# ReLU²-attention into a SwiGLU feed-forward on one core: last keys transposed apart, transposes and normalisation moved in the first batches

## The chip, the cores and the metric

The kernel runs on one core of a Trainium2 chip. The metric is the device time of one execution, in microseconds. The engines named below are TensorE (PE), VectorE (DVE), ScalarE (ACT), GpSimd (POOL, which here only issues loads) and SyncE (SP, which issues stores and transposing DMAs). Each engine executes its own instructions in program order and waits on semaphores for the others.

## The reference

Inputs are q, k, v of shape 8 x 12 x 448 x 64 (batch, heads, sequence, head size) and the weights of a feed-forward block with 768 model columns and 1536 hidden columns.

```python
scores = scale * np.matmul(q, k.transpose(0, 1, 3, 2))
attn = np.maximum(scores, 0.0) ** 2 / S
attn_out = np.matmul(attn, v)
x = attn_out.transpose(0, 2, 1, 3).reshape(B * S, H * D)
xn = x / np.sqrt(np.mean(x * x, axis=-1, keepdims=True) + 1e-06) * rms_g
g = xn @ w_gate
out = (g * sigmoid(g) * (xn @ w_val)) @ w_out
```

There is no softmax: the scores are cut at zero and squared.

## The kernel before

**Attention.** A stage `m` (0 to 23) handles four heads of one batch `b = m // 3`, as two pairs of heads; a head pair fills the 128 partitions of a transposed tile. Stages 0 to 2 are batch 0, stages 3 to 5 batch 1. `scores` (L266) makes seven score tiles per stage, called slots: slots 0 to 2 are keys 0 to 383 of the first pair in three chunks of 128, slots 3 to 5 the same of the second pair, and slot 6 holds the last 64 keys of both pairs. Each slot is a pair of 448-wide matmuls per head (into `psS`, two buffers), a ReLU on ACT (L291) and a square on DVE (L292). `attend` (L295) multiplies the seven squared tiles of the previous stage with the values, ACT copies the two results to `xT` (L327) and DVE squares them (L328).

**Transposes.** Scores need q and k with the head size on partitions. For the first two batches `transposes(n)` (L198) does that on PE for one head pair: fourteen small matmuls for q into `psQ` (where they are due), six for the 384 main keys and two for the last 64 keys into `psK`. DVE copies `psQ` to `QT` (L210) and `psK`, 448 wide, to `KT` (L223). A matmul of a slot waits until the copy that wrote its keys is done. From batch 2 on the keys (and from the second pair of batches on the queries too) come by transposing DMAs on SP, issued by the call with `j == 2`; for those batches `transposes` puts nothing else on PE beyond the q of batches 2 and 3.

**Feed-forward.** After the third stage of a batch its `norm` (L345) sums the squares with six matmuls into `psSS`, takes the root on ACT (L357), and appends to a list `bg` four reciprocals (L370) and six scalings to `xn` (L373) for DVE, and then the generation of the gate, value and output pieces. `fill` (L464) issues pieces of gates (L400, with SiLU on ACT, L408), values (L414, with a product on DVE, L421) and output projections (L443) between the slots of the attention, by a budget of time, one `bg` step with each piece.

**Order.** There is no planner: the loop at L483 writes the order out by hand, and each engine follows it. In stage `m`: slots 0 and 1; `attend(m-1)`; slots 2 and 3; fill; `norm` in stages 3, 6, 9 and so on; slots 4 and 5; `transposes(2m+2)`; fill; slot 6; `transposes(2m+3)`; fill. In stage 3 there is nothing to fill with yet, and all of `bg` is issued at the stage's end. In stages 1 to 3 `warm` (L260) puts two spare matmuls on a tile of ones ahead of each of the slots 2 to 5, one ahead of `attend`; eight stand at the start and eight in stage 4 after slots 0 and 1.

**PSUM.** `psQ`, `psK`, `psAV`, `psSS`, `psG`, `psV`, `psO` and the spare matmuls' tile take turns in four buffers with the tag `rot`.

**Loads.** POOL issues them in program order: heads 0-1 of q and k, then heads 2-3, 4-7 and 8-11, with the last 64 keys of all twelve heads (`load_kx`) ahead of the keys of heads 2-3.

Of the kernel before, what the change touches and what calls it, by code (L numbers as in the profile page):

```python
# [9 lines left out]
BF16 = mybir.dt.bfloat16  # L10
# [5 lines left out]
def kernel(  # L16
# [11 lines left out]
    nc = tc.nc  # L28
    P = nc.NUM_PARTITIONS

    B, H, S, D = q.shape
# [5 lines left out]
    XT0 = NCH * P  # L37
    XK = S - XT0
# [7 lines left out]
    ND = HP // 2  # L46
# [12 lines left out]
    psum = ctx.enter_context(  # L59
        tc.tile_pool(name="psum", bufs=2, space=bass.MemoryType.PSUM)  # L60
    )
# [15 lines left out]
    q_t, k_t, kx_t, v_t, vx_t = {}, {}, {}, {}, {}  # L77
# [14 lines left out]
    def load_q(pr, h0=0, h1=H, es=(0, 1)):  # L92
        for e in es:
            dst = q_t[pr][e * HALF : (e + 1) * HALF]
            src = q[2 * pr + e, h0:h1]
            if pr < 2:
                nc.gpsimd.dma_start(
                    out=dst[:, h0:h1],
                    in_=src.rearrange("h (p u) d -> p h u d", u=NU),
                )  # L100
            else:
                nc.gpsimd.dma_start(
                    out=dst, in_=src.rearrange("h (p u) d -> p u h d", u=NU)
                )

    def load_k(b, h0=0, h1=H):
        src = k[b, h0:h1, 0:XT0]
        if b < 2:
            nc.gpsimd.dma_start(
                out=k_t[b][:, h0:h1],  # L110
                in_=src.rearrange("h (p c) d -> p h c d", c=NCH),
            )
        else:
            nc.gpsimd.dma_start(
                out=k_t[b][:], in_=src.rearrange("h (p c) d -> p c h d", c=NCH)
            )

    def load_kx(b, h0=0, h1=H):
        nc.gpsimd.dma_start(
            out=kx_t[b][:, h0:h1], in_=k[b, h0:h1, XT0:S].rearrange("h p d -> p h d")  # L120
        )
# [15 lines left out]
    def load_gv(lo, hi):  # L137
        nc.gpsimd.dma_start(out=wg_sb[:, :, lo:hi], in_=wg_d[:, :, lo:hi])
        nc.gpsimd.dma_start(out=wv_sb[:, :, lo:hi], in_=wv_d[:, :, lo:hi])
# [6 lines left out]
    ident = const_pool.tile([P, P], BF16, name="ident", tag="ident")  # L146
    masks.make_identity(nc, ident[:])
    load_q(0, 2, 4, (0,))
    load_kx(0)
    load_k(0, 2, 4)  # L150
    load_v(0, 0, 4)
    eps_col = const_pool.tile([P, 1], FP32, name="eps_col", tag="eps_col")
    nc.vector.memset(eps_col[:], eps)  # L153
# [21 lines left out]
    def step():  # L175
        if bg:
            bg.pop(0)()


    QT, KTt, R, XT, X2 = {}, {}, {}, {}, {}  # L180
# [8 lines left out]
    def turn(dst, src, r0, r1):  # L189

        for hh in range(2):
            nc.tensor.transpose(  # L192
                out=dst[hh * D : (hh + 1) * D],
                in_=src(hh)[r0:r1],
                identity=ident[r0:r1, r0:r1],
            )

    def transposes(n):  # L198


        b, j = divmod(n, HP)
        pr, e = divmod(b, 2)
        if pr == 0 or pr == 1 and e == 0:
            r0, r1 = (e * HALF, (e + 1) * HALF) if pr == 0 else (0, P)
            if j == 0 and e == 0:
                big(pr, None)
            ps = psum.tile([P, NU, r1 - r0], BF16, name="psQ", tag="rot", bufs=4)
            for u in range(NU):
                turn(ps[:, u, :], lambda hh: q_t[pr][:, 2 * j + hh, u, :], r0, r1)
            nc.vector.tensor_copy(out=QT[pr][:, j, :, r0:r1], in_=ps[:])  # L210
        if b < 2:
            if j == 0:
                big(None, b)
            ps = psum.tile([P, S], BF16, name="psK", tag="rot", bufs=4)
            for c in range(NCH):
                turn(
                    ps[:, c * P : (c + 1) * P],
                    lambda hh: k_t[b][:, 2 * j + hh, c, :],
                    0,
                    P,  # L220
                )
            turn(ps[:, XT0:S], lambda hh: kx_t[b][:, 2 * j + hh, :], 0, XK)
            nc.vector.tensor_copy(out=KTt[b][:, j], in_=ps[:])  # L223
        if j == 2 and b > 0 and b + 1 < B:
            if e == 1 and pr > 0:
                big(pr + 1, None)
                for u in range(NU):
                    nc.sync.dma_start_transpose(
                        out=QT[pr + 1][:, :, u, :],
                        in_=q_t[pr + 1][:, u].rearrange("p h d -> p (h d)"),  # L230
                    )
            big(None, b + 1)
            for c in range(NCH):
                nc.sync.dma_start_transpose(
                    out=KTt[b + 1][:, :, c * P : (c + 1) * P],
                    in_=k_t[b + 1][:, c].rearrange("p h d -> p (h d)"),
                )
            nc.sync.dma_start_transpose(
                out=KTt[b + 1][:, :, XT0:S],
                in_=kx_t[b + 1][:].rearrange("p h d -> p (h d)"),  # L240
            )
        if j == HP - 1:
            if b + 2 < B:
                k_tile(b + 2)
                load_k(b + 2)
                load_kx(b + 2)
            if e == 0 and pr + 1 < B // 2:
                q_tile(pr + 1)
                load_q(pr + 1)
            if b == 0:  # L250
                load_gv(768, 1024)
                load_gv(1024, F)


    W: dict = {}

    def warm_tile():
        W["ps"] = psum.tile([P, S], FP32, name="psW", tag="rot", bufs=4)

    def warm(k):  # L260
        for _ in range(k):
            nc.tensor.matmul(  # L262
                out=W["ps"][:], lhsT=ones_bf[:, :P], rhs=ones_bf[:], start=True, stop=True
            )

    def scores(m, slots, k=0):  # L266
        b, t = divmod(m, ND)
        qt, kt = QT[b // 2], KTt[b]
        for s in slots:
            warm(k)  # L270
            ps = psum.tile([P, 2, 512], FP32, name="psS", tag="psS")
            if s < 2 * NCH:
                i, c = divmod(s, NCH)
                todo = [(2 * t + i, slice(0, P), slice(c * P, (c + 1) * P))]
            else:
                todo = [
                    (2 * t + i, slice(i * XK, (i + 1) * XK), slice(XT0, S))
                    for i in range(2)
                ]
            for j, rows, keys in todo:  # L280
                for hh in range(2):
                    prt = slice(hh * D, (hh + 1) * D)
                    nc.tensor.matmul(  # L283
                        out=ps[rows, hh, :S].rearrange("k (u x) -> k u x", u=NU),
                        lhsT=kt[prt, j, keys],
                        rhs=qt[prt, j, :, b % 2 * HALF : (b % 2 + 1) * HALF],
                        start=True,
                        stop=True,
                    )
            r = rpool.tile([P, 2, S], BF16, name="r", tag="r")  # L290
            nc.scalar.activation(out=r[:], in_=ps[:, :, :S], func=ACT.Relu)  # L291
            nc.vector.tensor_tensor(out=r[:], in0=r[:], in1=r[:], op=ALU.mult)  # L292
            R[m, s] = r
# [170 lines left out]
    def fill(us, idle_steps=3):  # L464

        nonlocal debt
        debt += us
        while pieces and debt > 0:
            cost, fn = pieces.pop(0)
            fn()  # L470
            debt -= cost
            step()
        if not pieces:
            debt = 0.0
            for _ in range(idle_steps):
                step()


    N = B * ND
    warm_tile()  # L480
    warm(8)
    transposes(0)
    for m in range(N + 1):  # L483
        rate = 7.8 if m < 2 * ND + 1 else 13.8
        first = m == ND
        idle = 2 if m <= ND else 0
        if m <= ND + 1:
            warm_tile()
        if m < N:
            scores(m, (0, 1))  # L490
        if m == ND + 1:
            warm(8)
            fill(0.36 * rate)
        if m > 0:
            warm(idle // 2)
            attend(m - 1)
        else:
            transposes(1)
        if m < N:
            scores(m, (2, 3), idle if m > 0 else 0)  # L500
        if not first:
            fill(0.36 * rate)
        if m > 0 and m % ND == 0:
            norm(m // ND - 1)
        if m < N:
            scores(m, (4, 5), idle if m > 0 else 0)
        if m + 1 < N:
            transposes(2 * m + 2)
        if not first:
            fill(0.36 * rate)  # L510
        if m < N:
            scores(m, (6,))
        if m + 1 < N:
            transposes(2 * m + 3)
        if first:
            while bg:
                step()
        else:
            fill(0.28 * rate)
    while pieces or bg:  # L520
# [31 lines left out]
```

## Time and profile before

| | |
|---|---|
| median of 3 runs | 476.93 us (476.84 to 477.58) |
| the profiled execution | 477.44 us, span 475.7 us |
| PE busy | 456.8 us, 96% of the span |
| DVE busy | 252.5 us, 53% |
| ACT busy | 253.6 us, 53% |
| spare matmuls (L262) | 43, 13.9 us busy |
| stage 1 begins (its slot 0 on PE) | 16.49 us |
| stage 2, stage 3, stage 4 begin | 26.04, 34.02, 43.95 us |
| first gate matmul | 48.69 us |
| `attend(3)` begins | 55.36 us |

How to read it: the profile is one execution. Its span is what the profile records, and its own time is 1.7 us more. A row of a timeline gives the start, the time from the first start to the last end of a run of like instructions, and in brackets the idle time before them with what ended it. A group's mean is the duration of one instruction; pipelined matmuls follow each other faster than that. The column PEclk is the granted clock of TensorE as a share of full speed.

### The profile page before, as it was taken

Reading aid. Unit: us, or ns where it says so; the run is one execution under the profiler, and the core shown is the slowest. Engines: PE = TensorE matmul, PEld = TensorE weight load, DVE = VectorE, ACT = ScalarE, POOL = GpSimd, SP = SyncE. Lnnn points to the kernel's source line nnn. Section 1 sums busy time; section 2 is a strip of 40 time slices with the busy share of each in tenths; the row PEclk is TensorE's granted clock in tenths of the full one; section 3 lists DMA queues with packets and bytes.
Section 4 is the critical chain, followed back from the end, with each engine's and each line's share of the span. In section 5 each row is a group of like instructions: output and inputs, shape, how many; then the busy total and the mean of one; then the engine's idle time right before and its main releaser. Section 6 shows DMA issues by size and latency. Waiting matters only on the chain.

```text
span 475.7 us, 7444 instructions
## 1 busy us (share of the span) xinstructions
PE 456.8 (96%) x3031; PEld 223.7 (47%) x3031; DVE 252.5 (53%) x428; ACT 253.6 (53%) x365; POOL 68.8 (14%) x75
## 2 busy tenths in 40 slices
PE   5988899979999999999999999999999999999996
PEld 2333344434455544444455544444455544555563
DVE  2677566785447555674446555674347552722111
ACT  3788266856474375666465375766465463422110
POOL 9653321510040003400040002000000000000000
PEclk9998899999999999999999999999999999999999
DMA  9999999999794216994294115500001210000022
GB/s 100 192 190 181 181 179 202 175 148 101 140 117 85 100 68 90 151 107 68 42 129 114 66 68 80 47 1 1 1 0 69 97 68 1 0 1 1 34 99 99
DMA packets 129282, 42.75 MB, mean 90 GB/s; under 512 B 113376, under 2 KB 125664, under 8 KB 129248
## 3 DMA queue, kind: packets, MB, share of 16 engines
q0 software_dynamic: 96336, 24.38, 61.0%
q1 hardware_dynamic: 32912, 17.90, 15.2%
q8 instruction: 23, 0.38, 0.3%
q14 instruction: 11, 0.09, 0.1%
HBM read 48.76 MB, written 11.01 MB: 126 GB/s over the span
## 4 chain that ended last, share of the span: by engine, by line
PE 86%; DVE 7%; ACT 4%; issue 1%; DMA 1%; POOL 0%; DVEq 0%; ACTq 0%; POOLq 0%
PE psO L443 23%; PE psV L414 22%; PE psG L400 22%; PE psS L283 8%; PE psAV L315 8%; ACT r L291 3%; DVE xn L373 2%; DVE r L292 2%; PE psSS L349 2%; DVE rstd L370 1%; DMA kxld<-in_k_dram 1%; PE psQ L192 1%; DVE QT L210 1%; PE psK L192 1%; DVE hT L421 1%
## 5 line engine op out<-in xcount | busy, mean ns | idle before, releaser
L291 ACT ACTIVATE r<-psS 128x896 bf16<-128x896 f32 x168 | 145.7, 921 | 39.9 <-PE psS L283 39.7
L292 DVE TENSOR_TENSOR r<-r 128x896 bf16<-128x896 bf16 x168 | 104.4, 624 | 92.3 <-ACT r L291 91.7
L400 PE MATMUL psG<-xn,wg_sb 128*128 128x448 bf16 x576 | 126.7, 353 | 4.2 <-DVE xn L373 4.1
L414 PE MATMUL psV<-xn,wv_sb 128*128 128x448 bf16 x576 | 125.9, 355 | 0.0
L443 PE MATMUL psO<-wo_sb,hT 128*128 128x384 bf16 x672 | 113.0, 326 | 0.0
L408 ACT ACTIVATE sig<-psG 128x448 bf16<-128x448 f32 x96 | 52.3, 546 | 111.5 <-PE psG L400 99.0
L421 DVE TENSOR_TENSOR hT<-sig,psV 128x448 bf16<-128x448 bf16 x96 | 59.1, 615 | 64.6 <-PE psV L414 63.1
L443 PEld LDWEIGHTS <-hT 128*128 128x128 bf16 x672 | 64.3, 98 | 46.1 <-issue 4.8
L400 PEld LDWEIGHTS <-wg_sb 128*128 128x128 bf16 x576 | 54.9, 98 | 57.7 <-issue 8.8
L414 PEld LDWEIGHTS <-wv_sb 128*128 128x128 bf16 x576 | 54.6, 98 | 56.1 <-issue 8.2
L283 PE MATMUL psS<-QT,KT 64*128 64x448 bf16 (+1 forms) x384 | 53.2, 372 | 7.2 <-DVE KT L223 4.3
L452 ACT COPY ost<-psO 128x384 f32<-128x384 f32 x28 | 13.4, 479 | 57.4 <-PE psO L443 50.3
L454 DVE COPY ost<-psO 128x384 f32<-128x384 f32 x28 | 15.6, 557 | 40.7 <-PE psO L443 40.7
L124 POOL DMA_DIRECT2D vld<-in_v_dram x10 | 9.6, 959 | 183.9 <-PE psAV L315 179.3
L283 PEld LDWEIGHTS <-KT 64*128 64x128 bf16 (+1 forms) x384 | 13.8, 97 | 40.6 <-issue 34.6
L315 PE MATMUL psAV<-r,vld 128*64 128x448 bf16 x288 | 32.8, 365 | 0.0
L373 DVE SCALAR_TENSOR_TENSOR xn<-xT,g_sb,rstd 128x448 bf16<-128x448 bf16 x48 | 31.0, 678 | 0.0
L327 ACT ACTIVATE xT<-psAV 128x448 bf16<-128x448 f32 x48 | 23.5, 542 | 4.6 <-PE psAV L315 4.4
L370 DVE RECIPROCAL rstd<-rstd 128x112 f32<-128x112 f32 x32 | 25.1, 822 | 0.0
L328 DVE TENSOR_TENSOR x<-xT 128x896 bf16<-128x896 bf16 x24 | 15.0, 625 | 15.0 <-ACT xT L327 15.0
L315 PEld LDWEIGHTS <-vld 128*64 128x64 bf16 x288 | 14.6, 111 | 16.3 <-issue 8.4
L262 PE MATMUL psW<-ones_bf 128*128 128x448 bf16 x43 | 13.9, 435 | 1.4 <-DVE eps_col L153 1.4
(34 smaller groups left out, 160.7 us busy)
## 6 DMA issues: line engine op xcount, KB each, us to landing
out_dram<-ost SPq DMA_DIRECT2D x28, 384.0 KB, 2.3
qld<-in_q_dram POOLq DMA_DIRECT2D x7, 672.0 KB, 16.8
kld<-in_k_dram POOLq DMA_DIRECT2D x7, 576.0 KB, 11.6
vld<-in_v_dram POOLq DMA_DIRECT2D x7, 576.0 KB, 7.2
wo_sb<-in_moe_w_out_dram POOLq DMA_DIRECT2D x3, 768.0 KB, 24.6
vxld<-in_v_dram POOLq DMA_DIRECT2D x16, 96.0 KB, 7.0
wg_sb<-in_moe_w_gate_dram POOLq DMA_DIRECT2D x4, 384.0 KB, 13.9
wv_sb<-in_moe_w_val_dram POOLq DMA_DIRECT2D x4, 384.0 KB, 14.1
```

What stands on the lines that cost most here:

```text
L283: nc.tensor.matmul(out=ps[rows, hh, :S].rearrange("k (u x) -> k u x", u=NU), lhsT=kt[prt, j, keys], rhs=qt[prt, j, :, b % 2 * HALF : (b % ...
L291: nc.scalar.activation(out=r[:], in_=ps[:, :, :S], func=ACT.Relu)
L292: nc.vector.tensor_tensor(out=r[:], in0=r[:], in1=r[:], op=ALU.mult)
L315: nc.tensor.matmul(out=acc[i][hh * D : (hh + 1) * D, :], lhsT=w[rows, hh, :], rhs=r[rows, hh, :], start=(c == 0), stop=(c == NCH),)
L327: nc.scalar.mul(out=xt[:, i, :], in_=acc[i][:], mul=inv_attn)
L370: nc.vector.reciprocal(out=rstd[:, sl], in_=rstd[:, sl])
L373: nc.vector.scalar_tensor_tensor(out=xn[:, kt, :], in0=xt[:, kt, :], scalar=g_sb[:, kt : kt + 1], in1=rstd[:], op0=ALU.mult, op1=ALU.mult,)
L400: nc.tensor.matmul(out=ps[:], lhsT=wg_sb[:, kt, fb * P : (fb + 1) * P], rhs=xn[:, kt, :], start=(kt == 0), stop=(kt == KT - 1),)
L408: nc.scalar.activation(out=sig[:], in_=ps[:], func=ACT.Silu)
L414: nc.tensor.matmul(out=ps[:], lhsT=wv_sb[:, kt, fb * P : (fb + 1) * P], rhs=xn[:, kt, :], start=(kt == 0), stop=(kt == KT - 1),)
L421: nc.vector.tensor_tensor(out=HT[pr, fb][:, :, e * HALF : (e + 1) * HALF], in0=st["sig"][:].rearrange("p (u x) -> p u x", u=NU), in1=ps[:] ...
L443: nc.tensor.matmul(out=ps[:], lhsT=HT[pr, fk][:, u, :], rhs=wo_sb[:, fk, o * OW : (o + 1) * OW], start=(fk == 0), stop=(fk == FT - 1),)
```

## The change

Six edits, all in how the first stages are ordered.

1. `psK` and its copy now hold only the 384 main keys. The last 64 keys of both pairs of a stage are transposed together by a new function `last_keys(m)`, into a tile `psX` (tag `rot`), and copied to `KT` by one more DVE copy. It is called in stages 0 to 5 after slots 4 and 5.
2. The load of the last 64 keys of batch 0 goes behind the keys of heads 2-3.
3. `transposes(2m+2)` goes ahead of slots 4 and 5 (in stage 0 it stays behind them).
4. In stage 3 the reciprocals and scalings are issued right behind the root, so ahead of the transposes, slots 4 to 6 and their squares.
5. In stage 4 the first fill (two gates and a value) goes ahead of slots 0 and 1.
6. Spare matmuls: two ahead of each of slots 0 to 5 in stage 0, none ahead of slots 4 and 5 in stage 3, four at the end of stage 3 in place of eight in stage 4; 47 in all.

```diff
     load_q(0, 2, 4, (0,))
+    load_k(0, 2, 4)
     load_kx(0)
-    load_k(0, 2, 4)
...
-            ps = psum.tile([P, S], BF16, name="psK", tag="rot", bufs=4)
+            ps = psum.tile([P, XT0], BF16, name="psK", tag="rot", bufs=4)
...
-            turn(ps[:, XT0:S], lambda hh: kx_t[b][:, 2 * j + hh, :], 0, XK)
-            nc.vector.tensor_copy(out=KTt[b][:, j], in_=ps[:])
+            nc.vector.tensor_copy(out=KTt[b][:, j, :XT0], in_=ps[:])
...
+    def last_keys(m):
+
+        b, t = divmod(m, ND)
+        ps = psum.tile([P, 2, XK], BF16, name="psX", tag="rot", bufs=4)
+        for i in range(2):
+            turn(ps[:, i, :], lambda hh: kx_t[b][:, 4 * t + 2 * i + hh, :], 0, XK)
+        nc.vector.tensor_copy(out=KTt[b][:, 2 * t : 2 * t + 2, XT0:S], in_=ps[:])
...
-        if m <= ND + 1:
+        if m <= ND:
             warm_tile()
+        if m == ND + 1:
+            fill(0.36 * rate)
         if m < N:
-            scores(m, (0, 1))
-        if m == ND + 1:
-            warm(8)
-            fill(0.36 * rate)
+            scores(m, (0, 1), idle if m == 0 else 0)
         if m > 0:
             warm(idle // 2)
             attend(m - 1)
         else:
             transposes(1)
         if m < N:
-            scores(m, (2, 3), idle if m > 0 else 0)
-        if not first:
+            scores(m, (2, 3), idle)
+        if first:
+            norm(0)
+            while bg:
+                step()
+        else:
             fill(0.36 * rate)
-        if m > 0 and m % ND == 0:
-            norm(m // ND - 1)
+            if m > 0 and m % ND == 0:
+                norm(m // ND - 1)
+        if m > 0 and m + 1 < N:
+            transposes(2 * m + 2)
+            if m < ND:
+                warm_tile()
         if m < N:
-            scores(m, (4, 5), idle if m > 0 else 0)
-        if m + 1 < N:
-            transposes(2 * m + 2)
+            scores(m, (4, 5), idle if m < ND else 0)
+        if m == 0:
+            transposes(2)
+        if m < 2 * ND:
+            last_keys(m)
         if not first:
             fill(0.36 * rate)
         if m < N:
             scores(m, (6,))
         if m + 1 < N:
             transposes(2 * m + 3)
         if first:
-            while bg:
-                step()
+            warm_tile()
+            warm(4)
         else:
             fill(0.28 * rate)
```

## The prediction

> **What bounds the kernel now.** I read the page first, then TensorE's waits, then the timeline of the first 60 us engine by engine, then the granted clock in short stretches.
>
> ```profile
> PE 456.8 (96%) x3031; PEld 223.7 (47%) x3031; DVE 252.5 (53%) x428; ACT 253.6 (53%) x365; POOL 68.8 (14%) x75
> ```
>
> ```profile
> PE psS L283 <- DVE KT L223: 4.3, 5, 1.1
> ...
> PE psK L192 <- DMA kxld<-in_k_dram: 1.9, 1, 1.9
> ```
>
> PE is the bound: 96% busy, and from 55 us on it hardly stops, so the end comes later by as much as PE enters that stretch later. The marker is `attend(3)`, at 55.36. Ahead of it PE waits five times for a KT copy (4.3 us) and once, at the start, for the last keys (1.9 us). The order of stages 2 and 3 on PE, DVE and ACT:
>
> ```profile
> 7.48 0.26 PE L192 MATMUL psK<-ident,kxld 64*64 64x64 bf16 x2 [1.89 <-DMA kxld<-in_k_dram]
> ...
> 26.04 0.55 PE L283 MATMUL psS<-QT,KT 64*128 64x448 bf16 x4 [0.83 <-DVE KT L223]
> ...
> 34.02 0.55 PE L283 MATMUL psS<-QT,KT 64*128 64x448 bf16 x4 [0.85 <-DVE KT L223]
> ...
> 41.88 0.38 PE L283 MATMUL psS<-QT,KT 64*64 64x448 bf16 x4 [0.41 <-ACT r L291]
> ...
> 43.95 0.93 PE L283 MATMUL psS<-QT,KT 64*128 64x448 bf16 x4 [1.03 <-DVE KT L223]
> ```
>
> ```profile
> 40.38 0.63 ACT L357 ACTIVATE rstd<-psSS,eps_col 128x448 f32<-128x448 f32 x1
> ...
> 43.51 0.38 DVE L223 COPY KT<-psK 128x448 bf16<-128x448 bf16 x1
> ...
> 44.94 2.98 DVE L370 RECIPROCAL rstd<-rstd 128x112 f32<-128x112 f32 x4
> 47.95 3.67 DVE L373 SCALAR_TENSOR_TENSOR xn<-xT,g_sb,rstd 128x448 bf16<-128x448 bf16 x6
> 51.53 1.16 DVE L292 TENSOR_TENSOR r<-r 128x896 bf16<-128x896 bf16 x2
> ```
>
> Slot 6 of stage 3 runs at 41.88, stage 4 begins at 43.95, and the normalisation, though its root is done at 41.01, is taken by DVE only at 44.94 and paces the first gate until 51.6.
>
> ```profile
> 44.00:48.00 4.00, 3.65 (x12) 1.19 (x13) 3.96 (x8) 3.01 (x3) 0.00 (x0) 0.60 1.72 182
> 48.00:51.00 3.00, 1.48 (x4) 0.38 (x4) 3.00 (x6) 0.00 (x0) 1.77 (x2) 0.94 1.27 201
> 51.00:54.00 3.00, 2.87 (x8) 1.09 (x8) 1.69 (x4) 0.54 (x1) 0.75 (x1) 0.50 1.36 175
> 54.00:56.00 2.00, 2.00 (x16) 0.91 (x16) 0.62 (x1) 0.53 (x1) 0.00 (x0) 0.99 1.51 152
> ```
>
> The columns are the stretch and its length, then busy time of PE, PEld, DVE, ACT and POOL, then the granted clock. It is 0.50 in 51 to 54, after a stretch with PE half idle, and 0.99 after 54. The pitch says the same: six value matmuls take 2.10 us of the chain at 52.20, six gate matmuls 1.14 at 54.30, so 0.36 against 0.19 us each. At the start the clock column shows 1.00, but matmuls have the slow pitch until 20.09 (eight spare ones in 3.17 us); there I go by the pitch.
>
> **The change part by part.** All times are of the profiled execution, 477.44 us (span 475.7), 0.5 above the median of 476.93.
>
> *Stage 0 (edits 1, 2, 6).* Slot 0 no longer waits for the last keys: the six main-key transposes end at 5.6, two spare matmuls (0.75) follow, the copy (about 0.35 against 0.38) is done by 6.0, so slot 0 is at 6.3 instead of 8.23. This lead of 1.9 us is lost: the keys of heads 4-7, issued at 6.67, land 6.4 us later at 13.07 (they ran at 14.43), and `transposes(2)` needs them. Behind it come the square of slot 5 and the copies QT, KT (0.30 each) and psX, then slot 6 at 14.9 (fast pitch) to 15.9 (slow), `transposes(3)` 0.6 to 0.97, and stage 1 begins at 15.8 to 16.9. I take 16.2, against 16.49. The swapped load costs nothing: the last keys land when the other load did, at 4.58 + 4.3 = 8.9, and are first needed near 13.4; without that slack `last_keys(0)` would wait up to 1.9, as before.
>
> *Stages 1 and 2 (edits 1, 3).* Let P be the beginning of a stage. As before, `attend` and two `xT` copies follow, the ReLU of slot 2 starts at P + 3.31 (26.04 to 29.35), and slot 3 leaves PE at P + 3.9. Now `transposes` (0.62 without last keys: 23.52 to 24.14) and two spares (0.48) come ahead of slot 4: P + 5.0, its ReLU at P + 5.4, 0.5 later than the spacing of 0.81 allows. The ReLU of slot 5 ends at P + 7.1. Slot 6 must now wait for the psX copy, which stands on DVE behind the square of slot 5: 0.03 + 0.62 + copy + 0.05, so P + 8.0. No row shows this copy of 128 columns; it lies between a 128x1 write (0.06) and the 448-wide copy (0.38), I take 0.2, nearer the copy. Then slot 6 (0.25) and `transposes(2m+3)` (0.62): the next stage begins at P + 8.9, where stage 2 took 7.98. What is saved is the wait of 0.83 for the KT copy; what replaces it is a PE wait of about 1.8 ahead of slot 6. Queued behind slot 6 on PE is everything, and ACT waits too.
>
> So with a fast clock stage 3 begins at 16.2 + 17.8 = 34.0, just as before (34.02). But the wait sits between two groups of transposes: from `transposes(2)` to stage 1 there are some 3.5 us with only slot 6 (0.25) as full matmuls; between stages 1 and 2 some 2.8. In the trace, 23.52 to 26.04 is such a stretch of 2.5 us and the pitch stays fast; 40.62 to 43.95 is one of 3.3 us and slots 0 and 1 come out slow (0.93 for four against 0.55). The first joint is longer than the one that dropped; I take a slow beginning of stage 1 and none after. Its price: `xT` came 20.50 - 16.49 = 4.01 after the beginning in slow stage 1 and 2.45 in stage 2, so 1.56 (bounds 0, and 2.4 if the spares ahead of slots 2 and 3 are slow too, about 0.4 for each pair). Stage 3 then begins at 35.6, 1.6 later (bounds -0.4 to +5).
>
> [...]
>
> *Stage 3 (edits 4, 6): the costly step.* Up to the root all stands as before, so it ends at 41.01 plus the delay. DVE then takes reciprocals and scalings at once (44.94 to 51.62 was 6.7): 47.7. Then come, in this order, QT and KT (0.6), the squares of slots 4 and 5 (1.16), and only then the psX copy (0.2): slot 6 runs at 49.7 instead of 41.88. ACT did its ReLUs long ago. PE has nothing to do from about 41 to 49.7 and is slow after it. Behind slot 6 are queued `transposes(9)` (0.51 + 0.46 slow, as at 9.09), four spares, two gates and a value (18 matmuls), slots 0 and 1 of stage 4. Slot 6 and transposes end at 51.1. All of xn is ready, so nothing paces the gates but the pitch. When does it become fast? The trace shows 3 us of dense matmuls (51 to 54), and 6.1 us from 13.92 to 20.0 with transposes among them; bounds 2.6 and 6, I take 4.3, their middle. At 0.37 that is 11.6 of the 22 matmuls; the other 10.4 at 0.19 take 2.0; slots 0 and 1 take 0.48: 51.1 + 4.3 + 2.0 + 0.5 = 57.9, against 55.36: 2.5 later (bounds 1.7 and 3.3). The eight spares of stage 4 and the wait for the scalings are gone in this sum; the stall has moved ahead of slot 6.
>
> *Stage 4 and later.* The ReLUs of slots 0 and 1 now stand behind the second SiLU (0.54 + two at 0.81), and slot 3 waits a little for its buffer: 0.1 (bounds 0 and 0.9, one ReLU). In stages 4 and 5 the chain to slot 6 is covered by three pieces (1.14 each) between `last_keys` and slot 6; without them it would cost the 0.9 of stage 2. Two of the moved q transposes of stages 6 to 8 (0.58 each) fall ahead of waits that exist anyway (1.39 for ACT at 98.36, 1.20 for the scalings at 102.11, whose DVE work stands in the same place): 0, bounds -0.5 and 0.5. On SP the transposing DMAs keep their sequence, on POOL only the swapped pair changes: 0; the latest gate weights land at 68.8 (40.97 + 27.8), 10 us ahead of their gate at 79.5. Six more DVE copies lie where DVE is idle, except as counted. The net of four more spares is in the sums.
>
> Sum: 1.6 + 2.5 + 0.1 = 4.2. 477.4 + 4.2 - 0.5 = 481.1.
>
> **The rivals.**
> *No slow beginning.* The clock holds between stages 0 to 3: 0.0 + 2.5 + 0.1 = 2.6, 479.5. For it: 23.52 to 26.04. Against: 43.95. [...]
> *More slow beginnings.* Stage 2 or 3 begins slow too, 1.56 each: 482.7 or 484.3. For it: 2.8 us is nearer to 3.3 than comfort; against: 2.5 held twice.
> *Faster.* The stages run at ACT's pace, because the moved copies take away the 0.91 us in which ACT waits for slot 0: 7.98 - 0.91 = 7.07 per stage. From 15.8 stage 3 would begin at 29.9, 4.1 earlier, and 4.1 - 2.6 is a gain of 1.5: 475.4. It decides if stage 3 begins before 31.4. Loads allow it (batch 1's keys land at 24.9). Against: slot 6 behind the square of slot 5, which no order on ACT can hide.
> *Small or no loss.* An early return of the fast clock in stage 3 (1.7) with part of that lead: 477 to 478.3.
>
> **How the numbers follow.** One slow beginning 0.40 (own range 479.9 to 482.4), none 0.25, more 0.22, a loss under 1.4 us 0.04, no measurable difference 0.03, faster 0.06. A measurement tells about 0.2%, 1 us, from no change. The range reaches from the no-drop case at its low norm stage and a little lead (478.3) to two further drops with a late clock (485.5); outside lie the faster, the equal and part of the small-loss case and the tail of the slow ones. Slower: 0.40 + 0.25 + 0.22 + 0.04 = 0.91.
>
> **What would show it.** Right: slot 0 near 6.3; a PE wait of 1.5 to 2 ahead of slot 6 in stages 1 and 2 put down to the psX copy; in stage 3 such a wait of 8 to 9 us, scalings done near 48 to 50; slow gates, `attend(3)` at 57 to 61. Wrong: if stage 3 begins before 31.4, or slot 6 of stage 3 doesn't wait, or PE has idle time after 60 us in which the delay vanishes.

## The result: 1.1% slower, as forecast

The changed kernel takes 481.80 us (median of 4 executions, 480.96 to 483.90), the kernel before 476.88 beside it. The ratio is 1.0108, with a 95% interval of 1.0073 to 1.0143. The forecast was 481.1, in 478.3 to 485.5. Here and below a ratio is taken over the executions that lie within 1.5% of the fastest of their kernel; this leaves out one execution of the sixth experiment and three of the tenth.

The profiled execution of the changed kernel is the slowest of its four: 483.90 us, span 482.1. So what is read from it is the costliest of four cases, 2.1 us above the median. For every execution the mean granted clock is known too; it is 0.978 in all four. The profiled execution stands 6.5 us above the profiled execution of before (477.44).

From its page, the engines' busy time, and TensorE's waits (in all, how often, the longest):

```profile
PE 458.3 (95%) x3035; PEld 223.8 (46%) x3035; DVE 252.9 (52%) x434; ACT 253.7 (53%) x365; POOL 68.8 (14%) x75
```

```profile
PE psS L290 <- DVE KT L259: 14.0, 4, 9.0
PE psG L407 <- DVE xn L380: 2.1, 3, 1.2
PE psS L290 <- ACT r L298: 1.8, 4, 0.9
```

PE's work has hardly grown (458.3 against 456.8). The wait for the last keys at the start and the waits of slot 0 for its keys are gone. One new line takes their place: four waits of slot 6 for the copy of the last keys (L259), 14.0 us, one of them 9.0. The timeline of PE shows where they are:

```profile
6.62 0.56 PE L290 MATMUL psS<-QT,KT 64*128 64x448 bf16 x2
...
15.64 0.38 PE L290 MATMUL psS<-QT,KT 64*64 64x448 bf16 x4 [1.65 <-DVE KT L259]
...
26.39 0.38 PE L290 MATMUL psS<-QT,KT 64*64 64x448 bf16 x4 [1.66 <-DVE KT L259]
...
27.21 0.36 PE L290 MATMUL psS<-QT,KT 64*128 64x448 bf16 x2
27.79 0.56 PE L290 MATMUL psS<-QT,KT 64*128 64x448 bf16 x2 [0.22 <-ACT r L298]
28.28 0.56 PE L269 MATMUL psW<-ones_bf 128*128 128x448 bf16 x1
28.77 2.45 PE L322 MATMUL psAV<-r,vld 128*64 128x448 bf16 x12
...
37.12 0.38 PE L290 MATMUL psS<-QT,KT 64*64 64x448 bf16 x4 [1.66 <-DVE KT L259]
...
37.94 1.14 PE L290 MATMUL psS<-QT,KT 64*128 64x448 bf16 x4
...
55.20 0.59 PE L290 MATMUL psS<-QT,KT 64*64 64x448 bf16 x4 [9.03 <-DVE KT L259]
```

Slot 0 runs at 6.62 instead of 8.23, but stage 1 begins at 16.46, where it began at 16.49. After each wait of 1.65 the next stage falls to the slow pitch: in stage 2 slot 0 is still fast (0.36 for two matmuls), slot 1 is slow (0.56), and the twelve matmuls of `attend` take 2.45 instead of 1.32. The same rows of the kernel before, in stages 1 and 2:

```profile
17.84 2.32 PE L315 MATMUL psAV<-r,vld 128*64 128x448 bf16 x12
...
26.82 1.32 PE L315 MATMUL psAV<-r,vld 128*64 128x448 bf16 x12
```

Stage 1 begins slow there too, at the end of the slow pitch from the start, so in stage 1 the drop takes away a gain and in stages 2 and 3 it is a loss against the kernel before. The granted clock of the changed kernel in stretches of the same execution (second column the length, then PE, PEld, DVE, ACT, POOL, then the clock):

```profile
16.60:20.00 3.40, 3.18 (x17) 1.08 (x14) 2.26 (x5) 2.02 (x3) 2.15 (x3) 0.64 1.31 205
...
26.80:30.20 3.40, 3.18 (x31) 1.31 (x27) 2.26 (x5) 2.54 (x3) 1.30 (x3) 0.65 1.55 194
...
37.00:40.00 3.00, 2.81 (x33) 1.24 (x35) 1.56 (x5) 2.42 (x3) 2.67 (x4) 0.67 1.46 196
...
51.00:54.00 3.00, 0.00 (x0) 0.00 (x0) 3.00 (x7) 0.00 (x0) 0.75 (x1) 0.50 1.43 145
```

In the kernel before the clock column of these early stretches is 1.00 up to 40 us (in its first 20 us that says little, because the column reads 1.00 at the slow pitch too, as in 6.4 to 9.8 us, where the four matmuls at 8.23 take 0.93). In 51 to 54 PE does nothing at all, and DVE is busy throughout; its timeline says with what:

```profile
46.69 2.99 DVE L377 RECIPROCAL rstd<-rstd 128x112 f32<-128x112 f32 x4 [1.32 <-ACT rstd L364]
49.71 3.67 DVE L380 SCALAR_TENSOR_TENSOR xn<-xT,g_sb,rstd 128x448 bf16<-128x448 bf16 x6
53.29 0.38 DVE L210 COPY QT<-psQ 128x448 bf16<-128x448 bf16 x1
53.59 0.35 DVE L222 COPY KT<-psK 128x384 bf16<-128x384 bf16 x1
53.86 1.15 DVE L299 TENSOR_TENSOR r<-r 128x896 bf16<-128x896 bf16 x2
54.92 0.22 DVE L259 COPY KT<-psX 128x128 bf16<-128x128 bf16 x1
```

The root ends at 46.65, the scalings follow without a gap, and the copy that slot 6 waits for comes last, 8.3 us after the root.

Four markers carry the rest of this section. Each is read from the profiled execution of its kernel; the experiments are described below.

| kernel | stages 1, 2, 3 begin | root ends | `attend(3)` begins | root to `attend(3)` | its time |
|---|---|---|---|---|---|
| before | 16.49, 26.04, 34.02 | 41.01 | 55.36 | 14.35 | 477.44 |
| changed | 16.46, 27.21, 37.94 | 46.65 | 62.25 | 15.60 | 483.90 |
| 1: normalisation late | 16.28, 27.04, 37.79 | 46.51 | 63.10 | 16.59 | 486.19 |
| 2: spares in the wait | 15.87, 25.16, 34.46 | 41.85 | 57.43 | 15.58 | 479.12 |
| 3: last keys early | 14.30, 21.73, 29.74 | 37.34 | 53.43 | 16.09 | 476.16 |
| 4: normalisation early alone | 16.59, 26.27, 34.26 | 41.25 | 57.49 | 16.24 | 481.76 |
| 5: copies first | 14.38, 22.66, 30.66 | 38.26 | 49.41 | 11.15 | 473.82 |
| 6: 5 with spares | 14.11, 21.50, 29.50 | 37.10 | 48.50 | 11.40 | 472.00 |
| 7: before, spares at the joint | 16.23, 26.22, 34.20 | 41.19 | 55.95 | 14.76 | 479.67 |
| 8: transposes in the wait | 16.11, 25.61, 35.12 | 42.50 | 58.51 | 16.01 | 480.17 |
| 9: stage 3 alone mended | 14.78, 24.52, 34.73 | 42.60 | 52.99 | 10.39 | 476.41 |
| 10: 6 with spares in the gate | 14.47, 21.86, 29.86 | 37.47 | 47.86 | 10.39 | 472.04 |
| 11: wait half filled | 15.76, 24.98, 34.20 | 41.58 | 58.71 | 17.13 | 483.05 |

Of the 6.9 us by which `attend(3)` is later in the changed kernel, 3.9 have come up by the beginning of stage 3, 1.7 more by the root (stage 3 begins slow too), and 1.25 between root and `attend(3)`. About 0.4 is given back by the end; the waits of stage 7 are 0.5 shorter, down from 1.39 + 0.44 + 1.20 + 0.25 to 0.88 + 0.44 + 1.17 + 0.25 us, because the q transposes now fill a part of the first.

### The profile page after: what moved, and what is told of

Its sections match the earlier page's. It is cut to its first block, busy times and chain, and to the rows that moved or that the text cites. A ratio compares the mean times of both kernels' runs of the same rounds, so it can differ in the third digit from the quotient of the medians.

```text
span 482.1 us, 7461 instructions
## 1 busy us (share of the span) xinstructions
PE 458.3 (95%) x3035; PEld 223.8 (46%) x3035; DVE 252.9 (52%) x434; ACT 253.7 (53%) x365; POOL 68.8 (14%) x75
## 4 chain that ended last, share of the span: by engine, by line
PE 89%; DVE 6%; ACT 3%; issue 1%; DMA 1%; POOL 0%; ACTq 0%; DVEq 0%; POOLq 0%
PE psO L450 23%; PE psV L421 22%; PE psG L407 22%; PE psS L290 8%; PE psAV L322 8%; ACT r L298 3%; DVE xn L380 2%; PE psSS L356 2%; PE psW L269 2%; DVE r L299 1%; DVE rstd L377 1%; PE psQ L192 1%; DMA kld<-in_k_dram 1%; PE psK L192 1%; DVE hT L428 0%
## 5 line engine op out<-in xcount | busy, mean ns | idle before, releaser
L322 PE MATMUL psAV<-r,vld 128*64 128x448 bf16 x288 | 35.0, 383 | 0.0
L322 PEld LDWEIGHTS <-vld 128*64 128x64 bf16 x288 | 15.2, 116 | 17.5 <-issue 10.5
L269 PE MATMUL psW<-ones_bf 128*128 128x448 bf16 x47 | 16.5, 454 | 1.4 <-DVE eps_col L153 1.4
```

Of the source, the lines that this page charges most:

```text
L269: nc.tensor.matmul(out=W["ps"][:], lhsT=ones_bf[:, :P], rhs=ones_bf[:], start=True, stop=True)
L322: nc.tensor.matmul(out=acc[i][hh * D : (hh + 1) * D, :], lhsT=w[rows, hh, :], rhs=r[rows, hh, :], start=(c == 0), stop=(c == NCH),)
```

## The experiments

The theory was that the copy of the last keys stands too far back in DVE's queue: behind the square of slot 5 in stages 0 to 2, where the wait then drops the clock, and behind the whole normalisation in stage 3. The rivals were that the place of the normalisation is the loss, that the clock drops for another reason, and that loads or ACT set the pace. Ratios are to the kernel before on the same chip.

### 1. Normalisation late again

```diff
         if first:
             norm(0)
-            while bg:
-                step()
...
         if first:
+            while bg:
+                step()
             warm_tile()
             warm(4)
```

> The changed kernel, but the reciprocals and scalings of stage 3 are again issued at the end of the stage. Theory (the last keys' copy, which slot 6 needs, is the cost; the normalisation only lengthens its queue): slot 6 of stage 3 waits about 2.5 us after the root instead of 8.6, but the reciprocals then start about 5 us after the root (3.9 in the kernel before), the gates are paced by the scalings again, and attend(3) begins 15 to 16 us after the root, as in the changed kernel (15.6). Time 481 to 483. Rival (putting the normalisation ahead is the whole loss): 477 to 478.

Measured: 484.15 us, ratio 1.0126 (1.0085 to 1.0168), above the expected 481 to 483. The long wait has shrunk and moved:

```profile
48.98 0.59 PE L290 MATMUL psS<-QT,KT 64*64 64x448 bf16 x4 [2.95 <-DVE KT L259]
...
55.52 3.42 PE L407 MATMUL psG<-xn,wg_sb 128*128 128x448 bf16 x6 [3.50 <-DVE xn L380]
```

Slot 6 waits 2.95 instead of 9.03, but now the gate waits 3.50 for its scalings, and they pace it. Taking the normalisation back alone regains nothing: from root to `attend(3)` it is 16.6 us, where 15 to 16 were expected. The rival falls.

### 2. Spare matmuls in the wait ahead of slot 6

```diff
+        if m < ND:
+            if m == 0:
+                warm_tile()
+            warm(9)
         if m < N:
             scores(m, (6,))
```

> The changed kernel with nine spare matmuls ahead of slot 6 in stages 0 to 2, in the 1.65 us in which PE waits there. Theory (that wait, with transposes on both sides, drops the clock, and each slow beginning costs about 1.6): stages 1 to 3 begin at the fast pitch, stage 3 begins near 34 to 34.5 instead of 37.9, time 479 to 480 with little spread. Rival (the clock drops for another reason, or a slow beginning costs nothing because ACT sets the pace): slow pitch stays or the time stays at 481 to 484.

Measured: 480.42 us, ratio 1.0041 (1.0027 to 1.0056), five executions within 1.5 us. All three stages begin fast:

```profile
25.16 0.36 PE L290 MATMUL psS<-QT,KT 64*128 64x448 bf16 x2
25.75 0.37 PE L290 MATMUL psS<-QT,KT 64*128 64x448 bf16 x2 [0.22 <-ACT r L298]
...
34.46 0.36 PE L290 MATMUL psS<-QT,KT 64*128 64x448 bf16 x2
35.05 0.36 PE L290 MATMUL psS<-QT,KT 64*128 64x448 bf16 x2 [0.22 <-ACT r L298]
```

Stages 1 and 2 take 9.3 us each instead of 10.7, so a slow beginning costs 1.4, and stage 3 begins at 34.46, 0.4 later than before. The other executions agree: the mean granted clock is 0.989 in all five, against 0.978 in all four of the changed kernel. Matmuls that compute nothing of use are worth about 0.7% here, so that part of the loss came through the clock.

### 3. Last keys ahead of slots 4 and 5

```diff
+        if m < 2 * ND:
+            last_keys(m)
+            if m == 0:
+                warm_tile()
         if m < N:
             scores(m, (4, 5), idle if m < ND else 0)
         if m == 0:
             transposes(2)
-        if m < 2 * ND:
-            last_keys(m)
```

> The changed kernel with the last keys transposed and copied ahead of slots 4 and 5 instead of behind them, in stages 0 to 5 (in stage 3 the normalisation still stands ahead of that copy). Theory: no wait ahead of slot 6 in stages 0 to 2, no slow beginnings, stages of about 7.2 us, stage 3 begins at 29.5 to 31; in stage 3 slot 6 still waits about 7.4 us after the root. Time 474 to 476. Rival (loads or ACT bind the stages, only the slow beginnings go): 478 to 479.

Measured: 476.46 us, ratio 0.9968 (0.9943 to 0.9993), ten executions from 474.68 to 480.27; the expected 474 to 476 is missed by a little. The wait is gone in stages 0 to 2 and stage 3 begins 4.3 us earlier than before. The rival on loads and ACT falls, but a part of it is right: stage 2 takes 8.0, not the 7.2 expected, and so no less than in the kernel before (7.98). The lead comes from stages 0 and 1. In stage 3 slot 6 still waits for the copy behind the normalisation, and from root to `attend(3)` it is 16.1:

```profile
44.81 0.59 PE L290 MATMUL psS<-QT,KT 64*64 64x448 bf16 x4 [7.96 <-DVE KT L259]
```

### 4. The kernel before with the normalisation early, and nothing else

```diff
             norm(m // ND - 1)
+        if first:
+            while bg:
+                step()
         if m < N:
             scores(m, (4, 5), idle if m > 0 else 0)
...
-        if first:
-            while bg:
-                step()
-        else:
+        if not first:
             fill(0.28 * rate)
```

> The kernel before with one part of the change alone: reciprocals and scalings of stage 3 right behind the root. Theory (what counts is which copy stands behind the normalisation on DVE): slot 6 doesn't wait, but slot 0 of stage 4 now waits for the key copy behind it, about 8.5 us after the root instead of 2.9; with the eight spares the first gate is near 12 us after the root and attend(3) about 15.5 after it instead of 14.35. Time 477.5 to 479. Rival (scalings 3.9 us earlier bring the gates forward by as much): 473 to 474.

Measured: 481.78 us, ratio 1.0074 (1.0059 to 1.0089); slower than I expected. The wait is as described, at slot 0 of stage 4:

```profile
49.70 0.93 PE L283 MATMUL psS<-QT,KT 64*128 64x448 bf16 x4 [6.55 <-DVE KT L223]
```

`attend(3)` comes 2.1 us later than before, yet the profiled execution takes 4.3 more. The rest is lost at the next normalisation, in stage 7: `attend(6)` is still 2.1 later (96.97 against 94.85) and `attend(7)` 4.2 (116.55 against 112.34). The clock there is 0.66, where the kernel before shows 1.00 (100 to 110 us; the first line is this kernel's, the second that of before).

```profile
100.00:110.00 10.00, 8.45 (x40) 3.52 (x40) 7.00 (x13) 3.85 (x6) 0.72 (x1) 0.66 2.44 134
```

```profile
100.00:110.00 10.00, 8.55 (x59) 4.25 (x58) 6.48 (x12) 3.18 (x5) 1.28 (x1) 1.00 2.59 153
```

So in this order too the early normalisation loses by the copy that PE needs soon and that stands behind it, and behind much the same waits for ACT in stage 7 (1.39 and 0.45 us here, 1.39 and 0.44 in the kernel before) the clock dropped here and didn't there.

### 5. Last keys early, and the copies of stage 3 ahead of the normalisation

```diff
         if first:
             norm(0)
-            while bg:
-                step()
...
         if m < 2 * ND:
             last_keys(m)
...
+        if first:
+            while bg:
+                step()
         if m < N:
             scores(m, (4, 5), idle if m < ND else 0)
```

(The call of `last_keys` stands as in the third experiment.)

> The changed kernel with the last keys ahead of slots 4 and 5 (as in the third experiment), and in stage 3 the copies of keys and queries ahead of the reciprocals, so that no PE instruction of attention waits behind the normalisation. Theory: slot 6 of stage 3 runs about 1 us after the root, the first gate matmul 3.7 us after it, attend(3) 10 to 12 us after it (16.1 in the third experiment): 4 to 6 us less than the third experiment's 474.7 to 476.5, so 469 to 472. Rival (PE is held in stage 3 by something other than the DVE queue, or the gain is given back in stage 7): 473 to 476.

Measured: 474.14 us, ratio 0.9926 (0.9900 to 0.9951). DVE now has the short copy done before the root is there:

```profile
37.46 0.21 DVE L259 COPY KT<-psX 128x128 bf16<-128x128 bf16 x1
38.30 2.99 DVE L377 RECIPROCAL rstd<-rstd 128x112 f32<-128x112 f32 x4 [0.63 <-ACT rstd L364]
41.32 3.66 DVE L380 SCALAR_TENSOR_TENSOR xn<-xT,g_sb,rstd 128x448 bf16<-128x448 bf16 x6
```

From root to `attend(3)` it is 11.15 us, as expected. The time is above the expected 469 to 472 and in the range of the rival (473 to 476), whose second half it bears out: `attend(3)` is 4.0 earlier than in the third experiment and the time only 2.3. `attend(6)` is still 4.0 earlier (89.42 against 93.44) and `attend(7)` 2.9 (107.47 against 110.40), so about 1.1 is given back in stage 7, where the clock is 0.79 in 92 to 100 us.

### 6. The same, with spare matmuls in three more waits

```diff
+        late = m == 2 * ND + 1
+        if late:
+            warm_tile()
         if m < N:
-            scores(m, (4, 5), idle if m < ND else 0)
+            scores(m, (4, 5), idle if m < ND else 2 if late else 0)
+        if late:
+            warm(5)
...
             warm_tile()
-            warm(4)
+            warm(9)
```

> The kernel of the fifth experiment with spare matmuls in three waits: nine at the end of stage 3 instead of four, two ahead of each of slots 4 and 5 of stage 7, and five before the fill that follows them, where the gates wait for the second normalisation. Theory (the spread of up to 5 us between executions comes from clock drops at such waits): the median falls by 0 to 2 us against the fifth experiment and the executions agree within 1.5 us. Rival (the spread comes from the loads): same spread, and 0 to 0.5 us slower by the spares.

Measured: 471.82 us, ratio 0.9864 (0.9803 to 0.9926); three executions within 0.5 us (471.52 to 472.00) and one at 480.06. The clock is 1.00 in stage 7. The median is 2.3 under the fifth experiment's, a little more than the expected 0 to 2, though the two intervals overlap. That the executions agree within 1.5 us is not met: the one at 480.06 was not profiled, and its 8 us are left open. Of the 1.8 us between the two profiled executions 0.9 is there at `attend(3)` already, from stages 0 and 1, where the two kernels are alike. `attend(7)` is 2.0 earlier (105.47 against 107.47), so the spare matmuls in stage 7 are worth about 1.1; those at the end of stage 3 bring nothing (from root to `attend(3)` 11.40 against 11.15).

### 7. The kernel before, with spares at the joint of stages 3 and 4

```diff
+        if m == ND + 1:
+            warm(8)
         if m < N:
             scores(m, (0, 1))
```

> The kernel before with eight more spare matmuls ahead of slots 0 and 1 of stage 4, in the wait of 1.03 us (eight fill 1.5). Theory (transposes and that wait drop the clock at 43.95): slots 0 and 1 come at the fast pitch (0.55 for four) about 0.5 later; the gates are paced by the scalings as before, but the first value group runs at 1.14 instead of 2.10, so attend(3) comes 0 to 1 earlier: 476.5 to 478. Rival (the drop has been decided before, by the waits near 41): 0.93 for four again.

Measured: 476.69 us, ratio 0.9987 (0.9962 to 1.0012), no difference that can be told.

```profile
45.43 0.55 PE L283 MATMUL psS<-QT,KT 64*128 64x448 bf16 x4
...
51.84 0.53 PE L400 MATMUL psG<-xn,wg_sb 128*128 128x448 bf16 x1 [0.25 <-DVE xn L373]
52.17 2.44 PE L414 MATMUL psV<-xn,wv_sb 128*128 128x448 bf16 x6
```

The drop at 43.95 is gone (0.55 instead of 0.93), so it did come from that joint. But the value group is slow all the same. Something between them drops the clock again. The likeliest is the gate whose matmuls each wait 0.25 us for a scaling; the tenth experiment tries that. `attend(3)` comes at 55.95, 0.6 later than in the kernel before, where 0 to 1 earlier was expected; this execution (479.67) is the slowest of the ten.

### 8. Transposes instead of spare matmuls in the wait

```diff
+        if m < ND:
+            dump = psum.tile([D, P], BF16, name="psD", tag="rot", bufs=4)
+            for _ in range(34):
+                nc.tensor.transpose(out=dump[:], in_=ident[:, :D], identity=ident[:])
         if m < N:
             scores(m, (6,))
```

> The changed kernel with 34 spare transposes (of the identity, into a tile that nobody reads) ahead of slot 6 in stages 0 to 2, in place of the nine spare matmuls of the second experiment; they keep PE busy for about the same 1.65 us. If transposes don't keep the clock up, stages 1 to 3 begin slowly as in the changed kernel: 481 to 484. If PE being busy is what counts, they begin at the fast pitch as with the spare matmuls: 479 to 480.5.

Measured: 480.73 us, ratio 1.0056 (1.0038 to 1.0074), ten executions from 479.63 to 481.25.

```profile
22.77 2.09 PE L530 MATMUL psD<-ident 128*64 128x128 bf16 x34
...
25.61 0.36 PE L290 MATMUL psS<-QT,KT 64*128 64x448 bf16 x2
26.19 0.37 PE L290 MATMUL psS<-QT,KT 64*128 64x448 bf16 x2 [0.22 <-ACT r L298]
...
26.79 1.33 PE L322 MATMUL psAV<-r,vld 128*64 128x448 bf16 x12
```

Fast, in all three stages, as with spare matmuls, and the mean granted clock is 0.989 in all ten executions. (The 34 take 0.4 longer than the wait was, and stages 1 and 2 take 9.5 us instead of 9.3.) The dense transposes kept the clock up here, so in these joints it was the idle PE that dropped it, and not the transposes around it.

### 9. Stage 3 alone mended

```diff
         if first:
             norm(0)
-            while bg:
-                step()
...
+        if first:
+            last_keys(m)
+            while bg:
+                step()
         if m < N:
             scores(m, (4, 5), idle if m < ND else 0)
...
-        if m < 2 * ND:
+        if m < 2 * ND and not first:
             last_keys(m)
```

> The changed kernel with stage 3 alone mended: there the last keys and the copies of keys and queries come ahead of the reciprocals; stages 0 to 2 keep the copy behind slot 5's square. Theory (the two losses are separate): stage 3 still begins 1.5 to 4 us later than in the kernel before, with slow beginnings, but attend(3) comes about 11 us after the root instead of 15.6: 476.5 to 479, some 4 us under the changed kernel. Rival (stage 3's wait is only the other stages' delay showing up): 480 to 482.

Measured: 478.81 us, ratio 1.0018 (0.9991 to 1.0045), ten executions from 475.19 to 481.58; not to be told from the kernel before, and 0.9% under the changed one. From root to `attend(3)` it is 10.4. Stages 2 and 3 begin slow after their waits:

```profile
23.17 0.59 PE L290 MATMUL psS<-QT,KT 64*64 64x448 bf16 x4 [1.65 <-DVE KT L259]
...
24.52 0.93 PE L290 MATMUL psS<-QT,KT 64*128 64x448 bf16 x4
```

Stage 1 comes behind a wait of only 0.73 in this execution and begins fast. So each loss can be mended without the other: filling the waits of stages 0 to 2 is worth 0.7% (second experiment), mending stage 3 alone 0.9%, some 3 to 4 us each. The ten executions differ by up to 6.4 us, and the time goes with the mean granted clock: 0.989 in the shortest, 0.970 in the two longest.

### 10. Spares between the matmuls of the first gate

```diff
             for kt in range(KT):
+                if b == 0 and fb == 0 and kt > 0:
+                    warm(1)
                 nc.tensor.matmul(
```

(On the kernel of the sixth experiment.)

> The kernel of the sixth experiment with one spare matmul ahead of each of the last five matmuls of the first gate, in the 0.25 us in which each waits for its scaling. Theory (the half-idle pacing there drops the clock, so that the first value group takes 2.24): the value group runs at 1.14, attend(3) about 1.3 earlier, 470 to 471. Rival (the clock is decided elsewhere): 471.5 to 472.

Measured: 473.22 us, ratio 0.9882 (0.9862 to 0.9903), eleven executions: eight from 470.76 to 474.40, three from 478.13 to 479.24.

```profile
43.65 0.35 PE L409 MATMUL psG<-xn,wg_sb 128*128 128x448 bf16 x1
43.83 0.35 PE L269 MATMUL psW<-ones_bf 128*128 128x448 bf16 x1
44.24 0.35 PE L409 MATMUL psG<-xn,wg_sb 128*128 128x448 bf16 x1
44.43 1.30 PE L423 MATMUL psV<-xn,wv_sb 128*128 128x448 bf16 x6
```

The value group is fast (1.30; 2.45 in the sixth experiment), so here the half-idle pacing was what dropped the clock. It doesn't always: in the ninth experiment four matmuls of the gate wait so (47.58 to 49.37), and the value group behind them is fast (1.29). The time doesn't follow: `attend(3)` is 0.64 earlier, but the profiled execution (472.04) is as long as that of the sixth (472.00), with PE waiting 5.5 us for ACT's ReLUs instead of 4.3; the expected 470 to 471 is reached by two of the eleven. This version can't be told from the sixth.

### 11. The wait ahead of slot 6 half filled

As the second experiment, with `warm(4)` for `warm(9)`.

> The second experiment with four spare matmuls ahead of slot 6 instead of nine, so that about 0.9 of the 1.65 us stay idle. The kernel before had joints of 0.83 us without a drop: by that the clock holds, 479 to 480.6 as with nine. If any wait in that place drops it: slow beginnings and 481 to 484.

Measured: 479.22 us, ratio 1.0036 (1.0018 to 1.0053), nine executions from 477.95 to 479.50 and one at 483.05.

```profile
24.16 0.38 PE L290 MATMUL psS<-QT,KT 64*64 64x448 bf16 x4 [0.79 <-DVE KT L259]
...
24.98 0.36 PE L290 MATMUL psS<-QT,KT 64*128 64x448 bf16 x2
25.56 0.36 PE L290 MATMUL psS<-QT,KT 64*128 64x448 bf16 x2 [0.22 <-ACT r L298]
```

An idle time of 0.79 in the same place didn't drop the clock, one of 1.65 did. Nine of the ten executions have the mean granted clock of the second experiment, 0.989. (The profiled execution is the one at 483.05; its stages begin fast, and it loses later, with the clock at 0.72 in 100 to 110 us.)

## Why the prediction was right, and where it was not

**Stage 0.** Slot 0 came at 6.62 for 6.3 and the lead was lost by stage 1 (16.46 for 16.2). The reason that I gave first, the landing of the keys of heads 4-7, held nothing up here: `transposes(2)` ran from 13.12 without a wait. (In eight of the experiments, where PE comes there sooner, it waits 0.3 to 0.8 us for these keys.) The lead went in the 1.65 us ahead of slot 6; the third experiment, without that wait, begins stage 1 2.2 ahead of the kernel before.

**Stages 1 and 2.** The wait ahead of slot 6 was forecast at about 1.8 and is 1.65. The length of a stage with a fast clock was put at 8.9 and is 9.2 to 9.3 (eleventh and second experiment). The likeliest case had one slow beginning at 1.56. The profiled execution has three, at 1.4 to 1.5 in stages 1 and 2 and 1.3 in stage 3 up to the root, so what happened is the rival "more slow beginnings", at 0.22, and not the likeliest case, at 0.40. The step "up to the root all stands as before" failed with it: stage 3 took 8.7 to the root instead of 7.0. For the rival 484.3 was worked out, against a median of 481.80. The other three executions are 1.7 to 2.9 us shorter than the profiled one, but their mean granted clock, which doesn't show the slow pitch of the start (the column reads 1.00 in the first 10.3 us of the profiled execution), is the same 0.978, so fewer drops behind the start don't explain it; where they are shorter isn't known.

**The reason for the drops was wrong.** The step measured a joint by its stretch with only slot 6 as full matmuls, and so left the transposes on both sides out of the count. In the eighth experiment 34 dense transposes (128 rows, 2.09 us) held the clock as nine matmuls did in the second; the mean granted clock is 0.989 in both. What fits these joints is idle time: waits of 0.73 to 0.85 between two stages didn't drop the clock (the kernel before, the ninth and the eleventh experiment), and waits of 1.65 did, in all eight places (three in the changed kernel, three in the first experiment, two in the ninth). In the changed kernel each slow stretch lasted 3.3 to 3.4 us, with a granted clock of 0.50 to 0.51.

The length of one wait doesn't decide it alone, though. In the kernel before the slow slots at 43.95 (0.93 for four matmuls) stand behind a wait of only 1.03. And the same wait of 1.35 ahead of slot 6 of stage 3 was followed by the fast pitch in the sixth experiment (nine spare matmuls in 1.88 us, from 38.79) and by the slow one in the ninth (four in 1.68, from 44.76, with a clock of 0.63 in 44 to 48):

```profile
37.96 0.38 PE L290 MATMUL psS<-QT,KT 64*64 64x448 bf16 x4 [1.35 <-ACT r L298]
```

```profile
43.45 0.54 PE L290 MATMUL psS<-QT,KT 64*64 64x448 bf16 x4 [1.35 <-ACT r L298]
```

These runs don't show what else decides it.

**Stage 3.** The mechanism was right: slot 6 behind the normalisation, 8.55 us after the root for 8.7, PE idle for 9.0 us. The term of 2.5 was too large for this execution. Root to `attend(3)` grew by 1.25, below the lower bound of 1.7, because the fast clock came back sooner: the first gate took 1.38 us and the value group 1.14, so the slow pitch ended about 2 us after the dense matmuls began, where I had taken 4.3, with 2.6 as the least. The size isn't fixed: in the eleventh experiment, whose stage 3 is the same, root to `attend(3)` is 17.13, 2.8 more than in the kernel before, because the slow pitch lasts through the first gate and most of the value group (2.45 and 1.97); in the second and the eighth it is 1.2 and 1.7 more. Two of the signs came later than forecast, because stage 3 began at 37.94: the scalings were done at 53.4 for 48 to 50, and `attend(3)` came at 62.25 for 57 to 61.

**The sum.** 1.6 + 2.5 + 0.1 was forecast. Measured in the profiled execution are 5.6 by the root, 1.25 behind it and 0.4 given back. In that execution the two wrong sizes offset each other only in part, 6.5 for 4.2. That the median lies 0.7 from the forecast is luck: the other executions are shorter for a reason that no term of the sum holds. The 0 for the q transposes of stages 6 to 8 was a gain of some 0.5, inside its bounds.

**The faster rival.** Its condition, stage 3 before 31.4, was met in the third experiment (29.74), and then a gain of 0.3% was there. But not by its mechanism: stages at ACT's pace of 7.07 were never seen, 8.0 was the least in stage 2.

**What stays open.** In the sixth and tenth experiments 4 of 15 executions lie 4 to 9 us above the others. None of them was profiled. The mean granted clock accounts for a part at most: in the sixth it is 0.989 against 0.996 to 0.998, but in the tenth executions of 473.50 and 478.13 us have the same 0.993.

## What to carry to other kernels

Before moving work up an in-order queue, list what then stands behind it and who waits for that: a copy of 0.22 us that stood behind the normalisation and two squares stopped TensorE for 9 us, and put ahead of them it stopped nothing; the same edits in that order are 0.7% faster than the kernel before, with spare matmuls 1.2 to 1.4%. On TensorE an idle time had a second price here, the clock after it: behind each wait of 1.65 us a stage began slowly, which cost 1.4 a stage in the changed kernel. A wait that can't be removed may be worth filling, and how long a wait is harmless has to be read from the trace: one of 1.35 was harmless in the sixth experiment and not in the ninth.

## What was not expected of the hardware

- A PE wait of 1.65 us was followed by the slow pitch in all eight places, in the changed kernel beginning 1 to 2 us after the wait and lasting 3.3 to 3.4 us (17.5 to 20.9, 27.9 to 31.2, 38.1 to 41.5, read from the pitch; the granted clock there is 0.50 to 0.51), in the ninth experiment with the matmuls right behind the wait (slot 6 in 0.59, where it takes 0.38 at the fast pitch). Waits of 0.73 to 0.85 between two stages were not, and one of 1.35 was in the ninth experiment and not in the sixth. A stretch that isn't idle but half busy (one matmul every 0.6 us, with 0.25 idle ahead of it, as in the first gate) was followed by it too in the seventh and sixth experiments (value group 2.44 and 2.45 us); with spares in it, in the tenth, the value group took 1.30, but in the ninth it took 1.29 without them.
- 34 dense transposes (2.09 us) held the clock up as nine matmuls (1.88 us) did: slot 0 of stage 2 takes 0.36 us behind both.
- The clock in and behind the waits of stage 7 dropped in some profiled executions and not in others: it is 0.66 in the fourth experiment (100 to 110 us), 0.79 in the fifth (92 to 100) and 0.72 in the eleventh (100 to 110, PE busy for 7.44 of it), and 1.00 in the kernel before and the changed one (100 to 110, PE busy for 8.55 and 7.26). Executions of one kernel spread by 6.4 us in the ninth experiment, where the time goes with the mean granted clock, and by 8.5 us in the sixth and the tenth, where it doesn't alone; so such drops don't make the whole spread.
